# Strassen's product for the values of token tiles 8 and 9, and x of the last token pair prepared a stage later

## The chip, the cores and the metric

The kernel runs on one core of one Trainium2 chip. The metric is the device time of one execution in microseconds: 639.72 us before the change, the median of three runs (639.28 to 639.74). Five engines work side by side, each from a queue of its own and in the order of that queue: TensorE (PE; the load of its weights is shown apart as PEld), VectorE (DVE), ScalarE (ACT), GpSimd (POOL) and SyncE (SP), which does nothing but issue transfers here. One instruction waits for another engine through semaphores, and whatever stands behind it in its queue waits too.

## The reference

2048 tokens of 640 numbers are normalized; a linear attention with 32 heads of 20 numbers and a feed-forward network of width 1536 both read the normalized tokens, and the result is x plus their product. All is float32.

```
xn  = layernorm(x)                                  # 2048 x 640
q, k, v = split(xn @ wqkv)                          # 32 heads of 20
pq, pk = q @ w_phi, k @ w_phi                       # per head
phi_q = concat(softmax(pq), softmax(-pq))           # 40 features of a head
phi_k = concat(softmax(pk), softmax(-pk))
kv  = einsum("bhsf,bhsd->bhfd", phi_k, v)           # sum over all tokens
z   = sum of phi_k over all tokens
s   = (phi_q @ kv) / (phi_q . z + 1e-6) @ wo
g   = silu(gelu(xn @ w1 + b1) @ w2 + b2)
out = x + s * g
```

## The kernel before, in words

The 2048 tokens are 16 tiles of 128. Two neighbouring tiles are a pair: pair q holds tiles 2q and 2q + 1. The 640 inputs of a token are five blocks of 128. A matrix product in float32 is made of three passes in a faster format: every operand is split into a high part (a copy of ACT) and a low part (value minus high part, on DVE or POOL), and PE multiplies high by high, high by low and low by high.

Phase 1 makes keys, values and queries. The key and query weights have `w_phi` folded in. Its plain form is a projection (`project`, matmuls at L401): one tile, five blocks, three passes and two halves of 320 columns, so 30 matmuls. The other form is Strassen's product for a whole pair (`token_pair`, matmuls at L714): blocks 0 and 1 of the even tile's and of the odd tile's inputs are combined beforehand, and so are the weights, and seven products with 54 matmuls give the result for both tiles. The list `QPARTS` (L686) is the order of the seven parts, i = 0 to 6; each ends with a copy on ACT or an addition on POOL or DVE that takes up its bank (L721 on POOL; L725, L728, L731 and L735 on DVE). The last part adds to the bank Z after DVE's addition of part 4 (L728) has read it, so its matmuls wait for that addition. After each part a hook can run, in which the caller places work of other engines: `hooks[i]` is called when part i has been written.

There is no scheduler: the code is written in the order in which each engine does its instructions. So a line that is moved in the code is moved in the queue of every engine that it uses.

A pair's x is prepared by these steps, each of which waits for the one before. `x_in` loads the tokens. `pair_stats` takes mean and variance on DVE (L220) and the power -1/2 on POOL (L223); SP stores mean and factor to DRAM (L326) and loads them back, spread over all partitions (L328, tile `bc`). `load_xr` loads the transposed x of the pair (`xr`, L252 and L253). `pair_sub` subtracts the mean on POOL (L335, two instructions), `pair_mul` multiplies by the factor on DVE (L340). Then `plain` splits it into the operand of the projections (`xp`, and `b` for two blocks of the odd tile; ACT L272, DVE L274, POOL L276). `t_sums` takes Strassen's sums of x (POOL L289, five instructions), and `t_split` splits them (`xd`; ACT L310, POOL L313).

A key or query passes from its bank through `feat1` (DVE: maximum L413, difference L416, minimum L419; POOL: the half with the other sign, L420) and `feat2` (exponential on ACT, L429). A query is then stored to DRAM. A key is finished by `key_fin`: sums and reciprocals on DVE (L437, L469), then the scaling on POOL (L442). `kv_pair` (L481) multiplies the finished keys of a pair with its values in 128 short matmuls, first those of the even tile; they take the heads nearly in order, and from the fourteenth matmul on they read the second half of that tile's values.

The loop from L762 runs over t = 6 to 9. Each turn has a key projection, a value projection and two query projections of tiles 0 to 7, and in turns 7, 8 and 9 the splits and sums of pairs 4, 5 and 6. In turn 9 `value_forms` (`vb`) splits the combined weights of the values that Strassen's product needs. The loop from L823 runs over p = 5, 6 and 7, which are tiles 10 to 15: two key projections, the key-value product of the pair before, and the values of the pair by Strassen's product (`value_pair`), with hooks. For p = 7, `forms` (`qf`) splits the combined query weights in the same way. Four pairs of queries follow by `token_pair` (pairs 4 to 7), and from 238.28 us on the feed-forward network.

Of the kernel before, what the change touches and what calls it, by code (L numbers as in the profile page):

```python
# [15 lines left out]
P = 128  # L16
# [30 lines left out]
def hedgehog_gated_mlp_kernel(ctx: ExitStack, tc: tile.TileContext, x, xt_in, wqk, bd, wv, wo, w1, b1, w2, b2, out_t):  # L47
# [259 lines left out]
    def t_split(q, later=False):  # L307
        dst = xd()[:, :, :, at(q)]
        tt = xrs.pop(q).rearrange("p k (o t) -> p (k o) t", o=2)[:, :9]
        nc.scalar.activation(dst[:, :, 0, :], tt, AF.Copy)  # L310

        def lo(o):
            nc.gpsimd.tensor_tensor(dst[:, o, 1, :], tt[:, o], dst[:, o, 0, :].bitcast(F32), op=OP.subtract)  # L313
        lo(slice(0, 5))
        if later:
            return lambda: lo(slice(5, 9))
        lo(slice(5, 9))
# [440 lines left out]
    XIN = {6: (12, 13), 7: (14, 15)}  # L758
    STATS = {6: (10, 11), 7: (12, 13), 8: (14, 15)}
    x_in(10)  # L760
    x_in(11)
    for t in range(6, 10):  # L762
# [5 lines left out]
        if t == 9:  # L768
            vb = value_forms(sv_raw, [nc.vector, nc.vector, nc.gpsimd, nc.gpsimd])
            next(vb)  # L770
            w_dump(0)
            w_dump(1)
# [3 lines left out]
        if t == 9:  # L776
            next(vb)
        if t > 6:
            feat2(es[t])
            pair_mul(q)  # L780
            pair_plain(q)
            t_sums(q)
        else:
            pair_sub(4)
            fold_w(wqT, range(4, KC), "wq", wq_s)
            feat2(es[t])
        vs[t] = value(t)
        phis[t] = key_fin(es.pop(t))
        pq = project(next(queries), wq_s)
        ef = feat1(pq)  # L790
        if t > 6:
            split_rest = t_split(q, t == 9)
            if t < 9:
                load_xr(q + 1)
        if t == 8:
            sv_raw = [load_raw(sv_dram[k]) for k in range(4)]
        if t == 9:
            next(vb)
# [7 lines left out]
        if t == 9:  # L806
            next(vb)
            next(vb)
            next(vb)
            split_rest()  # L810
            load_xr(7)
        if t in (7, 8):
            pair_sub(q + 1)
        if t < 9:
            store_e(queries_done.pop(0), ef)
        else:
            feat2(ef)
# [4 lines left out]
    qf, later, last_sums = None, [], []  # L822
    for p in range(5, 8):  # L823
# [6 lines left out]
        es[t] = feat1(pk)  # L830
        if p == 6:
            pair_mul(7)
        pk = project(t + 1, wk_s)
        kv_pair(t - 2)
        es[t + 1] = feat1(pk, later)
        if p == 6:
            plain(7, 0, xrs[7][:, :, :P])
            plain(7, 1, xrs[7][:, :, P:], slice(0, 1))
# [7 lines left out]
        def rest(t=t, p=p):  # L846
            if p == 5:
                nc.scalar.dma_start(e_dram[_tok(queries_done.pop(0))], ef)
                next(vb)
                next(vb, None)  # L850
            later.pop(0)()
            if p == 6:
                plain(7, 1, xrs[7][:, :, P:], slice(1, 2), False, True)
                t_sums(7)
            if p == 7:
                next(qf)

        def copied(t=t, p=p):
            feat2(es[t])
            if p == 7:  # L860
                next(qf)

        def first_key(t=t, p=p):
            phis[t] = key_fin(es.pop(t))
            feat2(es[t + 1])

        def second_key(t=t, p=p):
            if p < 7:
                phis[t + 1] = key_fin(es.pop(t + 1))
            else:  # L870
                phis[t + 1] = es.pop(t + 1)
                last_sums.append(key_sums(phis[t + 1]))
            if p == 6:
                t_split(7)

        value_pair(p, {0: lambda: p == 6 and plain(7, 1, xrs[7][:, :, P:], slice(1, 2), True, False), 1: rest, 2: copied, 3: lambda: p == 5 and pair_sub(7), 4: first_key, 6: second_key})
# [712 lines left out]
```

## Time and profile before

| | |
|---|---|
| median of three runs | 639.72 us |
| the profiled execution | 639.93 us |
| its span in the trace | 638.2 us |
| PE busy | 633.0 us, 99% |
| DVE busy | 510.5 us, 80% |
| POOL busy | 432.9 us, 68% |
| ACT busy | 260.5 us, 41% |
| granted clock of PE | nine tenths or more of full speed in each of the 40 slices |

The span runs from the first to the last instruction in the trace; the profiled execution has 1.7 us around it. Busy shares are means over the whole span; the page also cuts the span into 40 slices of about 16 us and shows the busy share of each in tenths. A timeline lists the instructions of one engine in order of time, one group a row: its start in the span, its length, line and operation, output and inputs by the names of the program, and shapes. In square brackets stands how long the engine had been idle before, and what released it.

### The profile page before, as it was taken

What the parts mean: (1) busy time and instruction counts of PE and PEld (TensorE: products, weight loads), DVE (VectorE), ACT (ScalarE), POOL (GpSimd) and SP (SyncE); (2) the same over time, 40 slices, a digit from 0 to 9 for tenths busy, and PEclk for the clock granted to TensorE, in tenths of its full rate; (3) what the DMA queues carried; (4) which work ended last, traced back from release to release, by engine and by line L of the source; (5) the groups of instructions that cost most, each with busy time, mean ns of one, the idle gap of its engine ahead of it and who ended that gap; (6) DMA issues with size and microseconds to landing.
All of it is one profiled execution on the core that took longest, in us unless ns stands there. A gap on an engine that the chain in (4) does not pass through costs nothing.

```text
span 638.2 us, 11443 instructions
## 1 busy us (share of the span) xinstructions
PE 633.0 (99%) x4330; PEld 552.0 (86%) x4330; DVE 510.5 (80%) x784; ACT 260.5 (41%) x389; POOL 432.9 (68%) x377
## 2 busy tenths in 40 slices
PE   9999999999999999999999999999999999999997
PEld 9999999999999998888888888888888888667676
DVE  5886976789788777878989869758798899887585
ACT  3622422334344257243442534842322335455540
POOL 1877466897977764987878776381735678857363
PEclk9999999999999999999999999999999999999999
DMA  8477287394411387449899699797498598969926
GB/s 346 121 234 226 70 286 222 93 299 148 157 43 45 135 273 274 141 95 357 213 280 317 162 368 346 154 318 257 143 238 171 168 187 264 305 184 322 346 71 198
DMA packets 167167, 136.89 MB, mean 214 GB/s; under 512 B 89864, under 2 KB 130824, under 8 KB 166728
## 3 DMA queue, kind: packets, MB, share of 16 engines
q1 hardware_dynamic: 164376, 124.56, 66.0%
q10 hardware_dynamic: 2736, 11.60, 4.8%
q8 instruction: 34, 0.56, 0.4%
q14 instruction: 21, 0.17, 0.1%
HBM read 87.76 MB, written 48.38 MB: 213 GB/s over the span
## 4 chain that ended last, share of the span: by engine, by line
PE 97%; DMA 2%; DVE 0%; SPq 0%; issue 0%; DVEq 0%
PE pB L988 26%; PE pA L401 24%; PE pB L959 23%; PE pB L1190 8%; PE pA L714 6%; PE pB L1116 2%; PE pA L164 2%; PE kv L481 2%; PE qV L714 1%; DMA phT<-phi_t 1%; PE qY L714 1%; DMA xres<-in_xt_dram 1%; PE pA L545 1%; PE pB L1098 0%; PE pA L387 0%; DVE y L1199 0%
## 5 line engine op out<-in xcount | busy, mean ns | idle before, releaser
L988 PE MATMUL pB<-hs,w2s 128*128 128x512 f32 x720 | 165.9, 389 | 0.0
L988 PEld LDWEIGHTS pB<-hs,w2s 128*128 128x128 f32 x720 | 135.0, 188 | 28.8 <-issue 0.8
L959 PE MATMUL pB<-xp,w1s 128*128 128x512 f32 x324 | 81.4, 389 | 0.0
L959 PE MATMUL pB<-xd,w1s 128*128 128x512 f32 x324 | 79.3, 389 | 0.0
L442 POOL TENSOR_TENSOR eq<-eq,rc 128x1280 f32<-128x1280 f32 x16 | 37.9, 2369 | 57.3 <-DVE rc L1050 40.1
L959 PEld LDWEIGHTS pB<-xp,w1s 128*128 128x128 f32 x324 | 60.7, 188 | 12.8 <-ACT x L975 0.3
L959 PEld LDWEIGHTS pB<-xd,w1s 128*128 128x128 f32 x324 | 60.8, 188 | 12.7
L997 DVE TENSOR_TENSOR y<-pB,y 128x512 f32<-128x512 f32 x100 | 63.1, 676 | 1.8 <-PE pB L988 1.8
L964 ACT ACTIVATE pB<-pB,b1t 128x512 f32<-128x512 f32 x48 | 31.8, 662 | 77.4 <-DVE pB L1387 28.9
L429 ACT ACTIVATE e<-e 128x1280 f32<-128x1280 f32 x32 | 40.7, 1273 | 50.1 <-POOL e L420 50.1
L401 PE MATMUL pA<-wk,xp 128*128 128x320 f32 x384 | 59.6, 310 | 0.0
L401 PEld LDWEIGHTS pA<-wk,xp 128*128 128x128 f32 x384 | 56.9, 188 | 0.1
L420 POOL TENSOR_TENSOR e<-nr,e 128x640 f32<-128x640 f32 x32 | 44.7, 1396 | 17.2 <-DVE nr L419 17.2
L1037 POOL TENSOR_TENSOR ez<-eq,zrep 128x1280 f32<-128x1280 f32 x16 | 47.4, 2963 | 6.5 <-DMA eq<-e_dram 6.5
L442 POOL TENSOR_TENSOR e<-e,rc 128x1280 f32<-128x1280 f32 x16 | 37.8, 2367 | 20.4 <-DVE rc L469 20.4
L401 PE MATMUL pA<-wv,xp 128*128 128x320 f32 x240 | 37.0, 310 | 0.0
L509 POOL TENSOR_TENSOR w1s<-raw,w1s 128x640 fp32r<-128x640 f32 (+1 forms) x18 | 25.4, 1412 | 16.0 <-ACT w1s L508 15.9
L139 POOL TENSOR_TENSOR w2s<-raw,w2s 128x640 fp32r<-128x640 f32 x23 | 36.1, 1592 | 0.2 <-ACT w2s L137 0.2
L401 PEld LDWEIGHTS pA<-wv,xp 128*128 128x128 f32 x240 | 35.5, 188 | 0.1
L970 DVE TENSOR_TENSOR hs<-pB,hs 128x512 fp32r<-128x512 f32 x48 | 32.0, 684 | 4.2 <-ACT hs L966 3.8
L137 ACT ACTIVATE w2s<-raw 128x640 fp32r<-128x640 f32 x24 | 17.2, 736 | 43.1 <-DMA xd_dram<-xhi 16.4
L413 DVE TENSOR_REDUCE mx<-pA 128x32 f32<-128x640 f32 x32 | 25.9, 809 | 10.1 <-PE pA L401 9.8
(219 smaller groups left out, 1269.7 us busy)
## 6 DMA issues: line engine op xcount, KB each, us to landing
raw<-in_w_dram SPq DMA_DIRECT2D x42, 320.0 KB, 5.1
e_dram<-e ACTq DMA_DIRECT2D x16, 640.0 KB, 3.9
eq<-e_dram SPq DMA_DIRECT2D x16, 640.0 KB, 5.8
phi_t<-eq SPq DMA_DIRECT2D x64, 160.0 KB, 3.3
phT<-phi_t SPq DMA_DIRECT2D x20, 512.0 KB, 7.5
xt<-in_x_dram SPq DMA_DIRECT2D x16, 320.0 KB, 6.2
xres<-in_xt_dram SPq DMA_DIRECT2D x20, 256.0 KB, 6.7
out_dram<-xres SPq DMA_DIRECT2D x19, 256.0 KB, 4.2
```

Of the source, the lines that this page charges most:

```text
L139: eng.tensor_tensor(sl[:, 1, :], raw, sl[:, 0, :].bitcast(F32), op=OP.subtract)
L401: nc.tensor.matmul(ps[:, hf, :HALF], stat_x(q, o, k, a), ws[k][:, b, hf * HALF:(hf + 1) * HALF], start=n == 0, stop=n == 3 * KC - 1)
L420: rest = lambda: nc.gpsimd.tensor_tensor(e5[:, :, :, 1, :], nr[:, :, :, None].to_broadcast([P, 2, 16, DH]), e5[:, :, :, 0, :], op=OP.subtract)
L429: nc.scalar.activation(ef, ef, AF.Exp)
L442: nc.gpsimd.tensor_tensor(e3, e3, rc[:, :, None].to_broadcast([P, 64, DH]), op=OP.mult)
L714: nc.tensor.matmul(bank[ch], q_x(blk, a, q), p_weight(base, f, w, k)[:, b], start=ch not in seen and n == 0, stop=n == len(mms) - 1, skip_ ...
L959: nc.tensor.matmul(bank[ch][:], tl[:, a, off + wo_:off + wo_ + P], mov(blk, b), start=new and n == 0, stop=n == len(mms) - 1, skip_group_c ...
L970: nc.vector.tensor_tensor(hs[:, 1], ps, hs[:, 0].bitcast(F32), op=OP.subtract)
L988: nc.tensor.matmul(ps[:], ws[i][:, b, d * P:(d + 1) * P], hs[o][i][:, a, :], start=i == n == 0, stop=(i, n) == (GF - 1, 2), skip_group_che ...
L997: nc.vector.tensor_tensor(y, ps[:], y, op=OP.add)
L1037: nc.gpsimd.tensor_tensor(zv, ef, zf, op=OP.mult)
L1190: nc.tensor.matmul(ps[:, mv], w, o[:, mv], start=first and n == 0, stop=last and n == len(steps) - 1, skip_group_check=True)
```

## The change

The values of tiles 8 and 9 are no longer made by two projections in the loop over t, but by a fourth use of `value_pair` at p = 5, behind the key projections of tiles 10 and 11; their key-value product follows it. For that the preparation of the two last pairs is laid out anew. Of pair 6, the multiplication, the splits and the sums go from t = 9 into the hooks of this value pair, and `t_split` and the load of pair 7 into the hooks of the next one. Of pair 7, the statistics (with their store and broadcast load) go from t = 8 into hooks 2 and 4 of the value pair of tiles 10 and 11, the mean subtraction behind it, and the multiplication ahead of the value pair of tiles 12 and 13. In that pair the key-value product of tiles 10 and 11 stands behind the first part. The keys of tiles 8 and 9 are finished a query later than before. At p = 7 the last two `next(qf)`, which split combined query weights, stand in hooks 4 and 5 in place of 1 and 2. Up to L313 line numbers of the two kernels agree; from L315 to L735 of the kernel before, those of the changed kernel are four lower.

The first piece is PE's queue from the key projection of tile 9 on, before. `wk_...` are the key's weights by blocks, `wv` and `wq_...` those of the values and queries, `xp` and `b_...` the split x.

```order
L401 MATMUL pA<-wk_216,xp 128x320 x6
L401 MATMUL pA<-wk_240,xp 128x320 x6
L401 MATMUL pA<-wv,b_1381 128x320 x12
L401 MATMUL pA<-wv,xp 128x320 x18
L401 MATMUL pA<-wq_854,xp 128x320 x6
```

After the change, PE goes from key 9 straight to the queries, and this stands behind the key projection of tile 11. `ws` are combined weights, `xd` Strassen's sums of x, `qY` and `qV` banks of the product, `kv` the bank of the key-value product.

```order
L397 MATMUL pA<-wk_240,xp 128x320 x6
L710 MATMUL pA<-wv,xp 128x320 x6
L710 MATMUL qY<-ws,xd 128x320 x6
L710 MATMUL pA<-wv,xp 128x320 x9
L710 MATMUL qV<-ws,xd 128x320 x6
L710 MATMUL qV<-wv,xp 128x320 x3
L710 MATMUL pA<-wv,xd 128x320 x15
L710 MATMUL pA<-ws,xp 128x320 x6
L710 MATMUL pA<-wv,xp 128x320 x3
L477 MATMUL kv<-e,v 32x40 x64
```

So the 60 matmuls of two projections are gone, 54 of a product have come, and the key-value product stands right behind them.

On DVE the piece before is the first value pair, of tiles 10 and 11. `qu` are the running sums of the product, `qV` and `pA` its banks, `v` the values, `rc` the reciprocals of a key.

```order
L725 TENSOR_TENSOR qu<-qu,qV 128x320
L728 TENSOR_TENSOR v<-qu,pA 128x16x20
L437 TENSOR_REDUCE rc<-e 128x64
L469 RECIPROCAL rc<-rc 128x64
L731 TENSOR_TENSOR v<-qu,pA 128x16x20
L735 TENSOR_TENSOR v<-qu,pA 128x16x20
```

After the change the first value pair is that of tiles 8 and 9, with `xr` and `bc` of pair 6.

```order
L721 TENSOR_TENSOR qu<-qu,qV 128x320
L724 TENSOR_TENSOR v<-qu,pA 128x16x20
L336 TENSOR_TENSOR xr<-xr,bc 128x1280
L727 TENSOR_TENSOR v<-qu,pA 128x16x20
L731 TENSOR_TENSOR v<-qu,pA 128x16x20
L274 TENSOR_TENSOR xp<-xr,xp 128x5x128
L274 TENSOR_TENSOR b_2039<-xr,b_2039 128x2x128
L274 TENSOR_TENSOR xp<-xr,xp 128x3x128
```

The multiplication of pair 6 now stands between the additions that complete the values, where the sums of a key stood in the pair before.

On POOL the piece is the value pair of tiles 10 and 11, before. `ws` are the last two split weights, `e` features, `nr` their minima.

```order
L721 TENSOR_TENSOR qu<-qx 128x320
L652 TENSOR_TENSOR ws<-raw,ws 128x320 x2
L420 TENSOR_TENSOR e<-nr,e 128x32x20
L335 TENSOR_TENSOR xr<-xr,bc 128x5x128 x2
L442 TENSOR_TENSOR e<-e,rc 128x1280 x2
L420 TENSOR_TENSOR e<-nr,e 128x32x20
```

And the same value pair after the change; `pst` are a pair's statistics.

```order
L717 TENSOR_TENSOR qu<-qx 128x320
L416 TENSOR_TENSOR e<-nr,e 128x32x20
L313 TENSOR_TENSOR xd<-xr,xd 128x5x128
L313 TENSOR_TENSOR xd<-xr,xd 128x4x128
L223 TENSOR_TENSOR pst<-pst,mhalf 128x1 x2
L438 TENSOR_TENSOR e<-e,rc 128x1280 x2
L331 TENSOR_TENSOR xr<-xr,bc 128x5x128 x2
L416 TENSOR_TENSOR e<-nr,e 128x32x20
```

The splits of pair 6's sums and the powers of pair 7's statistics have come into it, and the mean subtraction of pair 7 stands behind the scaling of the two keys, where it stood ahead of it.

The diff:

```diff
--- before.py
+++ after.py
@@ -304,17 +304,13 @@
         x_sums(lambda a, b: xr[:, a:b, :P], lambda a, b: xr[:, a:b, P:],
                lambda t: xt_two(xr.rearrange("p k (o t) -> p (k o) t", o=2), t))
 
-    def t_split(q, later=False):
+    def t_split(q, eng=nc.gpsimd):
         dst = xd()[:, :, :, at(q)]
         tt = xrs.pop(q).rearrange("p k (o t) -> p (k o) t", o=2)[:, :9]
         nc.scalar.activation(dst[:, :, 0, :], tt, AF.Copy)
 
-        def lo(o):
-            nc.gpsimd.tensor_tensor(dst[:, o, 1, :], tt[:, o], dst[:, o, 0, :].bitcast(F32), op=OP.subtract)
-        lo(slice(0, 5))
-        if later:
-            return lambda: lo(slice(5, 9))
-        lo(slice(5, 9))
+        for o, e in ((slice(0, 5), nc.gpsimd), (slice(5, 9), eng)):
+            e.tensor_tensor(dst[:, o, 1, :], tt[:, o], dst[:, o, 0, :].bitcast(F32), op=OP.subtract)
 
     def pair_stats(t):
         if t % 2 == 0:
@@ -755,8 +751,8 @@
     wq_f, wq_b, wv_f = [], [], []
     queries_done = list(range(NT // 2))
     queries = iter(range(NT // 2))
-    XIN = {6: (12, 13), 7: (14, 15)}
-    STATS = {6: (10, 11), 7: (12, 13), 8: (14, 15)}
+    XIN = {6: (12, 13), 9: (14, 15)}
+    STATS = {6: (10, 11), 7: (12, 13)}
     x_in(10)
     x_in(11)
     for t in range(6, 10):
@@ -767,34 +763,38 @@
             spill(3)
         if t == 9:
             vb = value_forms(sv_raw, [nc.vector, nc.vector, nc.gpsimd, nc.gpsimd])
-            next(vb)
             w_dump(0)
             w_dump(1)
         if t == 6:
             next(vf[1])
         es[t] = feat1(pk)
-        if t == 9:
-            next(vb)
         if t > 6:
             feat2(es[t])
-            pair_mul(q)
-            pair_plain(q)
-            t_sums(q)
+            if t < 9:
+                pair_mul(q)
+                pair_plain(q)
+                t_sums(q)
         else:
             pair_sub(4)
             fold_w(wqT, range(4, KC), "wq", wq_s)
             feat2(es[t])
-        vs[t] = value(t)
-        phis[t] = key_fin(es.pop(t))
+        if t < 8:
+            vs[t] = value(t)
+        if t < 8:
+            phis[t] = key_fin(es.pop(t))
         pq = project(next(queries), wq_s)
         ef = feat1(pq)
-        if t > 6:
-            split_rest = t_split(q, t == 9)
-            if t < 9:
-                load_xr(q + 1)
+        if t == 9:
+            pair_sub(6)
+        if t > 7:
+            phis[t] = key_fin(es.pop(t))
+        if 6 < t < 9:
+            t_split(q)
+            load_xr(q + 1)
         if t == 8:
             sv_raw = [load_raw(sv_dram[k]) for k in range(4)]
         if t == 9:
+            next(vb)
             next(vb)
         for u in STATS.get(t, ()):
             pair_stats(u)
@@ -804,22 +804,39 @@
         if t == 6:
             next(vf[1])
         if t == 9:
-            next(vb)
-            next(vb)
-            next(vb)
-            split_rest()
-            load_xr(7)
-        if t in (7, 8):
-            pair_sub(q + 1)
+            for _ in range(4):
+                next(vb)
+        if t == 7:
+            pair_sub(5)
         if t < 9:
             store_e(queries_done.pop(0), ef)
-        else:
-            feat2(ef)
         if t == 6:
             kv_pair(4)
         for u in XIN.get(t, ()):
             x_in(u)
     qf, later, last_sums = None, [], []
+
+    def x_last():
+        t_split(6)
+        load_xr(7)
+
+    def first_store():
+        feat2(ef)
+        next(vb)
+
+    def plain_hi(q):
+        for o in range(2):
+            plain(q, o, xrs[q][:, :, o * P:(o + 1) * P], lo=False)
+
+    def x_mid():
+        nc.scalar.dma_start(e_dram[_tok(queries_done.pop(0))], ef)
+        pair_mul(6)
+
+    def x_low():
+        plain(6, 0, xrs[6][:, :, :P], hi=False)
+        plain(6, 1, xrs[6][:, :, P:], hi=False)
+        t_sums(6)
+
     for p in range(5, 8):
         t = 2 * p
         pk = project(t, wk_s)
@@ -828,14 +845,15 @@
             qf = forms(sq_dram, wq_f, wq_b, [nc.vector, nc.vector, nc.vector, nc.gpsimd])
             next(qf)
         es[t] = feat1(pk)
+        pk = project(t + 1, wk_s)
+        if p > 6:
+            kv_pair(t - 2)
+        es[t + 1] = feat1(pk, later)
+        if p == 5:
+            value_pair(4, {1: first_store, 2: lambda: next(vb, None), 4: x_mid, 5: lambda: plain_hi(6), 6: x_low})
+            kv_pair(8)
         if p == 6:
             pair_mul(7)
-        pk = project(t + 1, wk_s)
-        kv_pair(t - 2)
-        es[t + 1] = feat1(pk, later)
-        if p == 6:
-            plain(7, 0, xrs[7][:, :, :P])
-            plain(7, 1, xrs[7][:, :, P:], slice(0, 1))
         if p == 7:
             next(qf)
             next(qf)
@@ -844,23 +862,30 @@
             wq_b.extend(wq_s[2:])
 
         def rest(t=t, p=p):
+            later.pop(0)()
+
+        def copied(t=t, p=p):
+            feat2(es[t])
             if p == 5:
-                nc.scalar.dma_start(e_dram[_tok(queries_done.pop(0))], ef)
-                next(vb)
-                next(vb, None)
-            later.pop(0)()
+                x_last()
+                pair_stats(14)
             if p == 6:
+                plain_hi(7)
+
+        def x_next(p=p):
+            if p == 5:
+                pair_stats(15)
+            if p == 6:
+                plain(7, 0, xrs[7][:, :, :P], hi=False)
+                plain(7, 1, xrs[7][:, :, P:], slice(0, 1), hi=False)
                 plain(7, 1, xrs[7][:, :, P:], slice(1, 2), False, True)
                 t_sums(7)
             if p == 7:
                 next(qf)
 
-        def copied(t=t, p=p):
-            feat2(es[t])
+        def first_key(t=t, p=p):
             if p == 7:
                 next(qf)
-
-        def first_key(t=t, p=p):
             phis[t] = key_fin(es.pop(t))
             feat2(es[t + 1])
 
@@ -870,10 +895,12 @@
             else:
                 phis[t + 1] = es.pop(t + 1)
                 last_sums.append(key_sums(phis[t + 1]))
+            if p == 5:
+                pair_sub(7)
             if p == 6:
                 t_split(7)
 
-        value_pair(p, {0: lambda: p == 6 and plain(7, 1, xrs[7][:, :, P:], slice(1, 2), True, False), 1: rest, 2: copied, 3: lambda: p == 5 and pair_sub(7), 4: first_key, 6: second_key})
+        value_pair(p, {0: lambda: p == 6 and kv_pair(10), 1: rest, 2: copied, 4: x_next, 5: first_key, 6: second_key})
     w1f = w1_forms(w1r)
 
     def early_rest(q, ea):
```

## Rows read from the trace of the kernel before

**Rows 1.** The page: busy time of each engine, and the DMA engines in 40 slices.

```profile
PE 633.0 (99%) x4330; PEld 552.0 (86%) x4330; DVE 510.5 (80%) x784; ACT 260.5 (41%) x389; POOL 432.9 (68%) x377
...
DMA  8477287394411387449899699797498598969926
```

**Rows 2.** Who PE waits for: us in total, times, longest.

```profile
PE pB L1116 <- DMA phT<-phi_t: 0.3, 1, 0.3
```

**Rows 3.** Timeline of PE: start us, length us, instructions, count.

```profile
119.48 4.67 PE L401 MATMUL pA<-wv,xp 128*128 128x320 f32 x30
...
123.98 4.56 PE L401 MATMUL pA<-wq,xp 128*128 128x320 f32 x30
...
128.38 1.92 PE L401 MATMUL pA<-wq,b 128*128 128x320 f32 x12
...
160.60 1.15 PE L714 MATMUL pA<-wv,xp 128*128 128x320 f32 x6
...
168.62 4.56 PE L401 MATMUL pA<-wk,xp 128*128 128x320 f32 x30
...
238.28 1.55 PE L959 MATMUL pB<-xp,w1s 128*128 128x512 f32 x6
```

**Rows 4.** Timeline of DVE, the same stretch.

```profile
129.93 1.48 DVE L437 TENSOR_REDUCE rc<-e 128x64 f32<-128x1280 f32 x1
...
131.91 0.76 DVE L413 TENSOR_REDUCE mx<-pA 128x32 f32<-128x640 f32 x1
...
134.30 0.88 DVE L220 BATCH_NORM_STATS2 st<-xt 128x6 f32<-128x320 f32 x2
...
143.94 1.26 DVE L652 TENSOR_TENSOR ws<-raw,ws 128x640 fp32r<-128x640 f32 x1 [1.99 <-ACT ws L648]
...
166.29 0.49 DVE L728 TENSOR_TENSOR v<-qu,pA 128x320 f32<-128x320 f32 x1
```

**Rows 5.** Timeline of POOL, the same stretch.

```profile
132.74 2.37 POOL L442 TENSOR_TENSOR e<-e,rc 128x1280 f32<-128x1280 f32 x1
...
136.30 2.83 POOL L313 TENSOR_TENSOR xd<-xr,xd 128x640 fp32r<-128x640 f32 x2
...
139.09 1.06 POOL L223 TENSOR_TENSOR pst<-pst,mhalf 128x1 f32<-128x1 f32 x2
...
140.12 1.28 POOL L420 TENSOR_TENSOR e<-nr,e 128x640 f32<-128x640 f32 x1
...
141.36 3.16 POOL L335 TENSOR_TENSOR xr<-xr,bc 128x640 f32<-128x640 f32 x2
...
149.52 3.87 POOL L289 TENSOR_TENSOR xr<-xr 128x256 f32<-128x256 f32 x5 [3.19 <-DVE xp L274]
...
164.79 0.87 POOL L721 TENSOR_TENSOR qu<-qx 128x320 f32<-128x320 f32 x1
...
165.63 1.72 POOL L652 TENSOR_TENSOR ws<-raw,ws 128x320 fp32r<-128x320 f32 x2
```

**Rows 6.** Timeline of ACT, one exponential.

```profile
141.43 1.27 ACT L429 ACTIVATE e<-e 128x1280 f32<-128x1280 f32 x1 [3.78 <-POOL e L420]
```

**Rows 7.** Timeline of DVE, three of the six multiplications of a pair.

```profile
63.24 1.49 DVE L340 TENSOR_TENSOR xr<-xr,bc 128x1280 f32<-128x1280 f32 x1 [3.68 <-POOL xr L335]
...
145.12 2.56 DVE L340 TENSOR_TENSOR xr<-xr,bc 128x1280 f32<-128x1280 f32 x1
...
175.67 3.26 DVE L340 TENSOR_TENSOR xr<-xr,bc 128x1280 f32<-128x1280 f32 x1
```

**Rows 8.** Timeline of SP: two stores of statistics, each with its broadcast load.

```profile
75.96 0.37 SPq L326 DMA_DIRECT2D st_dram<-pst  x1
...
79.17 0.32 SPq L328 DMA_DIRECT2D bc<-st_dram  x1
...
140.18 0.37 SPq L326 DMA_DIRECT2D st_dram<-pst  x1
...
146.69 0.32 SPq L328 DMA_DIRECT2D bc<-st_dram  x1
```

## The prediction

> **What bounds the kernel now.** I read the page first. TensorE (PE) is busy 633.0 of 638.2 us, 99% [rows 1]. Then who PE waits for: once it runs there is one wait, 0.3 us near the end [rows 2]. So the time is the sum of PE's instructions: a matmul less is its own length less, a wait of PE more is its own length more, and everything on the other engines is free as long as it ends before PE asks for it. Last I read, engine by engine, the stretch that the change rewrites (119 to 205 us) [rows 3 to 7], because there the other queues are nearly as full as PE's.
>
> **What it takes off PE.** Two value projections of 30 matmuls go, one token pair of 54 comes. A projection follows the one before it after 4.40 us (123.98 to 128.38), 0.147 us a matmul; a value pair takes 8.02 (160.60 to 168.62), of which 0.1 belongs to the key-value product just before it, since 54 x 0.147 is 7.92 [rows 3]. Saved: 8.80 - 7.92 = 0.88 us. The key-value products keep their number. Uncovered by any wait this gives 639.93 - 0.88 = 639.05 for the profiled execution, which stands 0.2 over the median 639.72.
>
> **What it puts on the path: the values of tiles 8 and 9.** PE's timetable without waits: queries 4 and 5 now start where the value projection of tile 8 stood, 119.5 [rows 3]; key 9 128.3, queries 6 and 7 132.7, keys 10 and 11 141.5, value pair 150.3 to 158.3, its last part (nine matmuls that add to a bank which VectorE, DVE, must have read) from 157.0, the key-value product of tiles 8 and 9 from 158.3. The other engines do the same work in less PE time, so I add up their queues.
>
> DVE is free at 129.9 [rows 4]. Features of a tile cost 2.4 (131.91 to 134.30), the sums with reciprocal of a key 2.0 (129.93 to 131.91). Query 4 ends 132.3, key 8's sums 134.3, then query 5, key 9, query 6: 141.5. GpSimd (POOL) has the pair sums done by 132.6 [rows 5]: half feature of query 4 (1.24), scaling of key 8 from 134.4 (2.37) to 136.8, two splits (2.8) 139.6, three half features (3.7) 143.3, the mean subtraction of pair 6 (3.15) 146.4. ScalarE takes key 9's exponential (1.27, [rows 6]) behind that of query 5 and a store, 142.5 to 143.8. DVE, idle till then, goes on: sums of key 9 145.8, a split of a weight form (1.2, [rows 4]) 147.0, query 7 149.4, another split 150.6, keys 10 and 11 155.4. Its first two additions for the values (0.5 each) end 156.4 [rows 4]. PE's last part needs that at 157.0: 0.6 to spare.
>
> Next in DVE's queue stands the multiplication of pair 6, and behind it the addition that completes the values of tile 8. Their key-value product reads that half from its fourteenth matmul on, 0.3 us in: 158.6. The multiplication took 1.49 with POOL at rest, 2.56 with one POOL instruction beside it, 3.26 with two [rows 7]: in the middle row 1.07 more for a half feature of 1.24. Here POOL's two splits (1.72 after an addition of 0.84, [rows 5]) end about 157.0, so 0.6 is shared. I scale the middle row: 0.5 more, 2.0, to 158.4, and 158.9 after the addition. PE waits 0.3; bounds 0 (1.49) and 1.6 (3.26).
> The Trainium skill (SBUF — State Buffer, Who interferes with whom) says that a DVE instruction with two SBUF inputs and a GpSimd one that reads SBUF block each other, the second for the whole of the first. The middle row agrees nearly: 1.49 and 1.24 make 2.73, it took 2.56. By the rule the multiplication is held until 157.0 and ends 158.5: PE would wait 0.4 instead of 0.3.
>
> **The statistics of the last pair.** They move from tile 8 into the next value pair, with their store, the broadcast load and the mean subtraction behind them. Pair sums began 1.84 after the multiplication's end at the like place (147.68 to 149.52) and took 3.87 [rows 5, 7]: 160.2 to 164.1. POOL goes on: clearing 0.3, addition 0.84 (165.2; DVE's two additions end 166.2, PE's last part of this pair comes at 166.7), half feature 166.5, splits 169.3, two powers (1.0) 170.3. The store and the broadcast that waits for it were issued 3.2 apart when little else ran (75.96 to 79.17) and 6.5 apart at 140.18, in a slice in which the DMA engines were nine tenths busy [rows 1, 8]. At 170 the load of pair 7 has landed (it waits in SyncE's queue, with this store behind it, for the buffer that query 7's store, issued about 155, gives back, so it goes out about 160), and the weight loads stand behind the broadcast, so I take 3.2: issued 173.6. No row shows the broadcast's landing by itself: between 3.2 and 6.5, taken 4.2, nearer the quiet row, 177.8. POOL has scaled keys 10 and 11 by 175.1. Subtraction 181.0, multiplication 2.6 (a half feature beside it) 183.6, two additions 184.6. PE: value pair 160.0 to 168.0 (0.3 late), keys 12 and 13 to 176.8, first part and the key-value product of 10 and 11, now inside the pair, to 179.1, last part 5.8 on, 184.9. So it just fits; I charge 0.1. Bounds: 0, with 1.3 to spare if both trips take 3.2, and 5.3 if both take 6.5. Keys 14 and 15 ask from 186.2 on for the split x that ends about 185.5, covered as long as the term above is.
>
> **The two splits of the query sums.** They go behind the fifth part of the last value pair, so DVE does the pair's two additions ahead of them (a gain that PE cannot use) and key 14's sums behind them. From that pair's start: second addition 6.0, two splits (1.26 each at most, [rows 4]) 8.5, addition 9.0, sums 11.0, POOL's scaling 13.3, its addition for the first query pair 14.2, DVE's two 15.2. PE's last part of that query pair starts at 8.0 + 6.7 = 14.7. Wait 0 to 0.5, taken 0.2, since the splits here are half as wide. The split weights themselves are asked for at 12.4 and 14.7, well after.
>
> Other moves cost nothing as far as rows go: the two token loads of pair 7 (now behind the weight dumps) have 20 us; banks for the projections, which come 4.4 and 8.8 earlier, are read by DVE 1.1 or more before the third projection after; pair 6's key projection starts at 168.0, its x ends about 162.
>
> **Sum.** -0.88 + 0.3 + 0.1 + 0.2 = -0.3: 639.6 for a profiled execution, 639.4 against the median.
>
> **Rivals.**
> 1. All is covered: POOL's splits end earlier and the multiplication takes 1.49. Then 639.05, against the median 638.8. For it: in the like place of before PE shows no wait at all. Against: two of the three rows have POOL beside the multiplication, and DVE has no idle time from 143.8 to 159.
> 2. Slower: the trip of the statistics through DRAM. Place: the last part of the third value pair behind DVE's multiplication of pair 7. Price: if the store alone takes the 6.5 of before's last trip, all is 3.3 later and PE waits 3.0 instead of 0.1: 642.3. It makes the kernel slower by more than 0.2% when store and broadcast together take over some 9.4 instead of 7.4. For it: that 6.5 is this kernel's own latest such trip. Against: what loaded the queues then is not there at 170.
> 3. POOL beside both multiplications throughout, 3.26 each: the key-value product waits 1.6, the later last part 0.4, the query pair 0.5: -0.88 + 2.5 = +1.6, 641.3.
> 4. The products save less or more than counted. PE's matmuls ran back to back in both forms, so I give it little.
>
> **Numbers.** Forecast 62%, rival 1 13%, rival 2 12%, rival 3 10%, rest 3%. About 0.2%, 1.3 us, is what a measurement of this kernel tells from no change. The forecast and rival 1 lie within it, since 0.88 us is 0.14%; rival 2 lies beyond, rival 3 on the border, half each. Faster 4%, within 79%, slower 17%. The range runs from rival 1 to just over rival 3: 638.7 to 641.6; the 5.3 us bound is left outside.
>
> **What would show it.** PE's rows: a token pair of 54 matmuls at about 150.3 and no projection of values after tile 7; the first FFN matmul, at 238.28 before [rows 3], 0.3 earlier. A wait of PE of 0 to 0.5 in the key-value product after that pair, released by DVE's addition, right behind a multiplication of about 2.0. The broadcast issued about 173.6 and the subtraction of pair 7 from about 178; if it starts after 180, PE's last part of the third pair waits and rival 2 holds. Wrong would be a wait at a place not named here, or a first FFN matmul more than 1.3 us from 238.3.

## The result and the profile after

The changed kernel takes 642.11 us (median of six runs, 641.33 to 642.95), the kernel before 639.77 beside it: a ratio of 1.0037, 95% interval 1.0024 to 1.0050. A second series gave 641.12 against 639.29, 1.0030 (1.0018 to 1.0043). The change makes the kernel slower by about 2 us. The forecast was 639.4; the first series lies outside its range (638.7 to 641.6), the second inside.

The page and the list of PE's waits after the change, to be held against [rows 1, 2]:

```profile
PE 632.6 (99%) x4324; PEld 550.7 (86%) x4324; DVE 511.8 (80%) x788; ACT 260.0 (41%) x390; POOL 435.8 (68%) x378
```

```profile
PE pA L710 <- DVE v L724: 1.4, 1, 1.4
PE pB L1143 <- DMA phT<-phi_t: 0.9, 1, 0.9
...
PE pB L1143 <- DVE r L1242: 0.2, 1, 0.2
PE kv L477 <- DVE v L727: 0.2, 1, 0.2
```

PE has six matmuls less, and once it runs four waits where it had one. The largest, 1.4 us, is in the last part of the third value pair, and the last is that of the key-value product of tiles 8 and 9. The two of L1143 are some 32 us from the end (608.2 and 609.4 of 641.0), in code that the change doesn't touch. PE's timeline (start, length, instructions, count) shows the two waits of values and product in place, and the start of the feed-forward network (FFN); the last fence is the key-value product of tiles 6 and 7 before:

```profile
119.02 4.66 PE L397 MATMUL pA<-wq,xp 128*128 128x320 f32 x30
...
157.93 0.47 PE L477 MATMUL kv<-e,v 128*32 128x40 f32 x26
158.57 1.20 PE L477 MATMUL kv<-e,v 128*32 128x40 f32 x102 [0.17 <-DVE v L727]
159.70 1.14 PE L710 MATMUL pA<-wv,xp 128*128 128x320 f32 x6
...
182.43 2.36 PE L710 MATMUL pA<-wv,xd 128*128 128x320 f32 x15
186.16 1.14 PE L710 MATMUL pA<-ws,xp 128*128 128x320 f32 x6 [1.37 <-DVE v L724]
...
239.08 1.55 PE L986 MATMUL pB<-xp,w1s 128*128 128x512 f32 x6
```

```profile
118.15 1.39 PE L481 MATMUL kv<-e,v 128*32 128x40 f32 x128
```

From the end of the key-value product of tiles 6 and 7 to the first FFN matmul it is 239.08 - 119.02 = 120.06 us; before, 238.28 - 119.48 = 118.80 [rows 3]. So this stretch, which holds the whole change, is 1.26 longer. It is cut into three: the product starts again after 1.77 (157.93 to 159.70) where it took 1.32 (118.15 to 119.48 in the profile before), 0.4 more; the last part starts 3.73 after the part ahead of it (182.43 to 186.16), where 15 matmuls of 0.147 are 2.20, 1.5 more and 0.1 in its first row; and 0.88 less for the six matmuls. That is about 1.2. Both waits cost PE some 0.3 more than the idle time that the list gives (1.6 against 1.37, and 0.4 against 0.17): rows overlap where PE doesn't wait (the 15 matmuls are listed with 2.36), and the first row behind a wait is 0.1 longer.

What was late there, on SP, POOL and DVE:

```profile
169.91 0.37 SPq L322 DMA_DIRECT2D st_dram<-pst  x1
173.22 0.33 SPq L324 DMA_DIRECT2D bc<-st_dram  x1
```

```profile
178.56 3.13 POOL L331 TENSOR_TENSOR xr<-xr,bc 128x640 f32<-128x640 f32 x2 [4.01 <-DMA bc<-st_dram]
181.63 1.28 POOL L416 TENSOR_TENSOR e<-nr,e 128x640 f32<-128x640 f32 x1
182.85 0.17 POOL L447 MEMSET v<- 128x32 f32 x1
...
183.11 1.89 POOL L717 TENSOR_TENSOR qu<-qx 128x320 f32<-128x320 f32 x1
```

```profile
181.72 2.55 DVE L336 TENSOR_TENSOR xr<-xr,bc 128x1280 f32<-128x1280 f32 x1 [2.46 <-POOL xr L331]
185.03 0.49 DVE L721 TENSOR_TENSOR qu<-qu,qV 128x320 f32<-128x320 f32 x1 [0.76 <-POOL qu L717]
185.62 0.49 DVE L724 TENSOR_TENSOR v<-qu,pA 128x320 f32<-128x320 f32 x1
```

The store of pair 7's statistics and its broadcast went out almost when the forecast had them (173.2 against 173.6). The subtraction that waits for the broadcast began 5.3 later. The multiplication took 2.55, as forecast. But POOL's addition, 0.87 alone [rows 5], took 1.89: it stood until the multiplication had ended at 184.27. The clearings ahead of it, which read nothing, ran in 0.17 and less under the same multiplication. DVE's two additions came behind POOL's, at 186.1.

The page gives the loss of one execution; 1.26 us of the stretch do not make 2 us. The table sets the profiled executions side by side: the stretch, and the rest from the first FFN matmul to the end of the execution.

| execution | stretch | from the FFN's start to the end | time |
|---|---|---|---|
| before, three executions | 118.80, 118.81, 118.77 | 401.65, 401.56, 401.07 | 639.93, 640.06, 639.15 |
| changed kernel, five | 120.06, 120.06, 119.89, 119.71, 119.89 | 403.60, 402.54, 401.95, 402.84, 403.06 | 642.68, 641.61, 641.29, 641.65, 642.02 |

On average the stretch is 1.13 longer and the rest 1.37; what comes ahead of the stretch is 0.4 shorter. The second loss was not in the forecast.

### The profile page after: what moved, and what is told of

Read it like the earlier page. It is cut to its first block, busy times and chain, and to the rows that moved or that the text cites. A ratio compares the mean times of both kernels' runs of the same rounds, so it can differ in the third digit from the quotient of the medians.

```text
span 641.0 us, 11437 instructions
## 1 busy us (share of the span) xinstructions
PE 632.6 (99%) x4324; PEld 550.7 (86%) x4324; DVE 511.8 (80%) x788; ACT 260.0 (41%) x390; POOL 435.8 (68%) x378
## 4 chain that ended last, share of the span: by engine, by line
PE 93%; POOL 2%; DMA 2%; DVE 1%; issue 0%; ACT 0%; DVEq 0%; SPq 0%; POOLq 0%; ACTq 0%
PE pB L1015 26%; PE pB L986 23%; PE pA L397 21%; PE pB L1217 9%; PE pA L710 6%; PE pB L1143 2%; PE pA L164 2%; PE qV L710 1%; PE kv L477 1%; PE qY L710 1%; DMA xres<-in_xt_dram 1%; DMA bc<-st_dram 1%; PE pA L541 1%; POOL xr L289 1%; DMA st_dram<-pst 1%
## 5 line engine op out<-in xcount | busy, mean ns | idle before, releaser
L993 ACT ACTIVATE hs<-pB 128x512 fp32r<-128x512 f32 x48 | 28.8, 600 | 2.1
L397 PE MATMUL pA<-wq,xp 128*128 128x320 f32 x192 | 29.6, 310 | 0.0
```

The lines of the kernel that those rows point to most:

```text
L397: nc.tensor.matmul(ps[:, hf, :HALF], stat_x(q, o, k, a), ws[k][:, b, hf * HALF:(hf + 1) * HALF], start=n == 0, stop=n == 3 * KC - 1)
```

## The experiments

Each kernel is the changed one with the edit shown, if nothing else is said. Ratios are to the kernel before, timed beside it.

**The changed kernel again** (e1_again, and three executions more).

> The changed kernel once more, for a second profile. Of its 2.3 us over the kernel before, the stretch from the end of the key-value product of tiles 6 and 7 to the first FFN matmul explains 1.26 (120.06 against 118.80 us); PE waits 1.4 in the last part of the third value pair there. Theory A (the statistics of pair 7 come too late, all else is chance of one execution): the stretch is again 119.9 to 120.3, and what lies behind the first FFN matmul comes out near that of before (401.65 us from there to the end of the execution) in some executions, so the median is 641.0 to 641.5. Theory B (the change also lengthens something behind the FFN's start, by 1 us or more, through other transfers): the rest is again 403 or more and the median 642.

1.0030 (1.0018 to 1.0043), stretch 120.06, rest 402.54: the time, 641.12, and the stretch are those of theory A, and the rest lies between the two theories, 0.9 over that of before. The further executions were to tell whether the trip through DRAM varies:

> The changed kernel a third time, one execution with its profile. Over the kernel before it takes 1.8 to 2.3 us more, and only 1.26 of it lie in the stretch up to the FFN in the two profiles so far; executions spread over 640.3 to 644.0, those of the kernel before over 638.5 to 640.5. Theory C (the trip of pair 7's statistics through DRAM takes a different time in each execution and now shows in PE's wait): the stretch and the wait vary from execution to execution, 120 to 122 us, with the time from the issue of the store to the landing of the broadcast. Theory B (the rest is lost at the end, in the last transfers): the stretch is 120.0 to 120.1 each time, and the part behind the FFN's start varies, 402.5 to 404.

Stretch 119.89, 119.71, 119.89; store to broadcast 2.9 to 3.2, broadcast to subtraction 5.3 to 5.5. Theory C fell: the trip is steady. The stretches lie 0.1 to 0.3 below what either theory said. The rest varied from 401.95 to 403.06, nearly as B said (402.5 to 404). Two executions of the kernel before, taken for their profiles (e4_before and e8_before), gave the rows of the table. They too were to tell how far the rest varies: theory A had up to 1 us, theory B under 0.4. The first of them lay 0.1 under the first profile, the second 0.6, more than B gave.

**Powers ahead of the splits** (e2_pow).

```diff
             if p == 5:
-                x_last()
+                load_xr(7)
                 pair_stats(14)
+                pair_stats(15)
...
             if p == 5:
-                pair_stats(15)
+                t_split(6)
```

> Changed kernel, with the statistics of tile 15 taken right behind those of tile 14 and the two splits of pair 6's sums put behind them, so that POOL's two powers stand ahead of the splits (2.8 us). Theory A: the store and the broadcast of pair 7 go out 2.5 to 2.8 us earlier (about 170.5 instead of 173.2), the subtraction starts about 175.7, the multiplication ends by 182, PE's wait of 1.4 in the last part of the third value pair is gone, the stretch to the FFN is 118.4 to 118.6 and the time 1.6 us under the changed kernel. Rival (the wait comes from the multiplication and GpSimd blocking each other there, not from the late broadcast): the multiplication still stands beside GpSimd instructions, the wait stays over 1 us and the time is within 0.5 us of the changed kernel.

The same rows on SP, POOL and DVE:

```profile
167.12 0.37 SPq L322 DMA_DIRECT2D st_dram<-pst  x1
170.12 0.33 SPq L324 DMA_DIRECT2D bc<-st_dram  x1
```

```profile
175.32 3.14 POOL L331 TENSOR_TENSOR xr<-xr,bc 128x640 f32<-128x640 f32 x2 [0.78 <-DMA bc<-st_dram]
178.42 1.28 POOL L416 TENSOR_TENSOR e<-nr,e 128x640 f32<-128x640 f32 x1
...
180.52 1.26 POOL L717 TENSOR_TENSOR qu<-qx 128x320 f32<-128x320 f32 x1 [0.58 <-ACT qx L716]
```

```profile
179.19 1.86 DVE L336 TENSOR_TENSOR xr<-xr,bc 128x1280 f32<-128x1280 f32 x1
182.72 0.49 DVE L721 TENSOR_TENSOR qu<-qu,qV 128x320 f32<-128x320 f32 x1 [1.67 <-PE qV L710]
```

All came 2.8 to 3.2 earlier, DVE's addition now waits for PE, and PE's wait is gone. Stretch 118.28 (expected 118.4 to 118.6), 639.76 against 641.12 (1.4 less, 1.6 expected): 1.0009 (1.0000 to 1.0017). Theory A held for this wait. POOL's addition was still held here (1.26 instead of 0.87), but with 3 us more to spare nothing waited for it.

**The key-value product later as well** (e3_powkv, on the kernel of e2_pow, and once more as e16_powkv).

```diff
-            kv_pair(8)
...
-        value_pair(p, {0: lambda: p == 6 and kv_pair(10), ...
+        value_pair(p, {0: lambda: p < 7 and kv_pair(2 * p - 2), ...
```

> As the run before, and the key-value product of tiles 8 and 9 put behind the first part of the next value pair, so that PE reaches it 0.9 us later. Theory A: PE's wait behind the multiplication of pair 6 (0.2 us, and 0.3 more in which the product's matmuls start slowly) goes too: the stretch to the FFN is 118.0, 0.8 under the kernel before. If nothing is lost behind the FFN's start, the time is 0.6 to 0.9 us under the kernel before (638.9 to 639.2); if theory B holds and 1 us or more is lost there, it is 0.2 to 1 us over it.

> The kernel of the third experiment a second time, for its gain over the kernel before: 0.47 us there, with a stretch 0.81 shorter. Theory A alone: 0.8 under the kernel before; with some of the loss at the end, 0.2 to 0.6 under it again.

The first series: stretch 117.99, 638.82 against 639.29, 0.9991 (0.9982 to 1.0000). The second: 118.46, 639.30 against 639.12, 1.0002 (0.9993 to 1.0010). The stretch is that of the saving alone, 0.81 less, in one execution; in the other POOL ran 0.4 later in the first value pair, and PE lost 0.5 in the last parts of two pairs. The second series missed both expectations, which lay under the kernel before. This is the best variant, and it is not measurably faster than the kernel before.

**The half feature away from the multiplication** (e5_half).

```diff
-        es[t] = feat1(pk)
+        es[t] = feat1(pk, later if p == 6 else None)
...
             later.pop(0)()
+            if p == 6:
+                later.pop(0)()
...
+            if p == 6:
+                plain_hi(7)
             feat2(es[t])
...
-            if p == 6:
-                plain_hi(7)
```

> Changed kernel, where in the third value pair POOL's half feature of key 12 no longer stands beside DVE's multiplication of pair 7, but behind POOL's addition (the high splits of pair 7 go ahead of key 12's exponential so that nothing later is held up). The broadcast is as late as before. Theory A with blocking (while DVE multiplies, a POOL instruction on the same memory stands still, and the other way round; each adds its whole length to the other): the multiplication takes 1.5 instead of 2.55 us, the addition ends at its end plus 0.84, PE waits 0.9 less (0.1 to 0.5 instead of 1.0 to 1.4) and the stretch to the FFN is 119.1 to 119.2 instead of 120.06. Rival (no blocking, only the late broadcast counts): the additions come no earlier, the stretch stays at 120.06.

DVE and POOL in the third value pair:

```profile
181.18 1.49 DVE L336 TENSOR_TENSOR xr<-xr,bc 128x1280 f32<-128x1280 f32 x1 [1.97 <-POOL xr L331]
183.44 0.49 DVE L721 TENSOR_TENSOR qu<-qu,qV 128x320 f32<-128x320 f32 x1 [0.77 <-PE pA L710]
```

```profile
178.00 3.14 POOL L331 TENSOR_TENSOR xr<-xr,bc 128x640 f32<-128x640 f32 x2 [3.51 <-DMA bc<-st_dram]
...
181.33 2.07 POOL L717 TENSOR_TENSOR qu<-qx 128x320 f32<-128x320 f32 x1
183.37 3.10 POOL L416 TENSOR_TENSOR e<-nr,e 128x640 f32<-128x640 f32 x2
```

PE's wait there is gone. The half feature, now behind POOL's addition, no longer slows the multiplication, which took 1.49. The addition began under it and took 2.07: it stood until 182.67 and then needed 0.73. So each of the two is held for as long as the other, begun first, still runs. The Trainium skill (SBUF — State Buffer, Who interferes with whom) says that a VectorE instruction with two inputs in SBUF, the on-chip memory of these tiles, contends with a GpSimd one that reads SBUF, that the shared port is an exclusive lock, and that the order of issue decides who blocks. The trace agrees in both directions: 2.55 for a multiplication behind a half feature, 1.89 and 2.07 for an addition behind a multiplication. Not all of the gain is the half feature's: DVE's two additions ended at 184.52 instead of 186.11, 1.06 by the shorter multiplication and 0.54 because the broadcast was that much earlier in this execution (subtraction from 178.00 instead of 178.56). PE asked for them at 184.58, so with the broadcast as late as before some 0.5 of the wait would have stayed (an estimate), as expected. The stretch is 119.69, not 119.1: 0.5 was spent further on, in waits of 0.6 for the split sums of pair 7 and 0.2 for a key, both on POOL, which does the same work later. The times do not show the gain: 1.0044 (1.0031 to 1.0057), and the profiled execution (640.02) is the shortest of the six.

**Statistics where they were** (e6_early).

```diff
-    XIN = {6: (12, 13), 9: (14, 15)}
-    STATS = {6: (10, 11), 7: (12, 13)}
+    XIN = {6: (12, 13), 7: (14, 15)}
+    STATS = {6: (10, 11), 7: (12, 13), 8: (14, 15)}
...
-                pair_stats(14)
...
-            if p == 5:
-                pair_stats(15)
```

> Changed kernel with the statistics of pair 7 back in the stage of tile 8, where the kernel before had them, and all else of the change kept. Theory A: the wait in the third value pair goes (-1.6), but in the stage of tiles 8 and 9, where the two value projections no longer give DVE 8.8 us of PE's time, DVE's 2.3 us more make PE wait some 1.5 for a bank before query 5 or 6, and the first addition chain of the value pair comes later: stretch to the FFN 119.6 to 120.4, about as the changed kernel. Rival (DVE had room there, and moving the statistics was needless): 118.2 to 118.5 and 1.6 us under the changed kernel.

```profile
138.72 2.00 PE L397 MATMUL pA<-wq,b 128*128 128x320 f32 x12 [1.37 <-DVE e L412]
```

The row is PE's: it waits 1.37 for a bank that DVE empties too late, the wait of the third pair is gone, and the stretch is 120.53, 0.1 over what theory A said: 1.0049 (1.0033 to 1.0064). So the move bought something: without the two projections DVE has no room for the statistics in that stage.

**The splits of the query weights back** (e7_splits, on the kernel of e3_powkv), and moved alone in the kernel before (e13_b_splits).

```diff
             later.pop(0)()
+            if p == 7:
+                next(qf)
...
             feat2(es[t])
+            if p == 7:
+                next(qf)
...
-            if p == 7:
-                next(qf)
```

> The kernel of the third experiment (stretch 117.99), with the last two splits of the combined query weights back behind the first and second part of the last value pair. The prediction put 0 to 0.5 us of wait on their move, taken 0.2; the profile of the changed kernel shows none. Theory A: the stretch stays at 118.0 within 0.1, and the time with it. Rival (the move was worth something, since DVE is freed for the last pair's additions): PE waits at the last part of that pair and the stretch is 118.3 or more.

> The kernel before, with only the last two splits of the query weights moved behind the fourth and fifth part of the last value pair (the last edit of the change by itself). Both theories: the stretch up to the FFN is 118.8, since nothing of it is on PE's path. Theory D (the end of the kernel hangs on transfers, and any difference in order shifts them; the kernel before happens to lie well): the time is 0.4 to 1.5 us over the kernel before all the same. Theory E (the loss behind the FFN's start belongs to the Strassen part or to its lateness): the time is that of the kernel before within 0.3.

DVE in the last value pair with the splits back, PE there, and then the same place of PE in e3_powkv:

```profile
199.19 1.16 DVE L648 TENSOR_TENSOR wqb<-raw,wqb 128x320 fp32r<-128x320 f32 x1
200.28 1.56 DVE L648 TENSOR_TENSOR ws<-raw,ws 128x320 fp32r<-128x320 f32 x1
201.76 0.47 DVE L721 TENSOR_TENSOR qu<-qu,qV 128x320 f32<-128x320 f32 x1
202.34 0.49 DVE L724 TENSOR_TENSOR v<-qu,pA 128x320 f32<-128x320 f32 x1
```

```profile
200.46 2.36 PE L710 MATMUL pA<-wv,xd 128*128 128x320 f32 x15
202.88 1.14 PE L710 MATMUL pA<-ws,xp 128*128 128x320 f32 x6
203.86 0.60 PE L710 MATMUL pA<-wv,xp 128*128 128x320 f32 x3
```

```profile
200.26 2.36 PE L710 MATMUL pA<-wv,xd 128*128 128x320 f32 x15
202.47 1.04 PE L710 MATMUL pA<-ws,xp 128*128 128x320 f32 x6
203.34 0.60 PE L710 MATMUL pA<-wv,xp 128*128 128x320 f32 x3
```

The list of waits shows nothing there, but PE needs 3.40 (200.46 to 203.86) where it needed 3.08, since DVE's second addition ends at 202.83, behind the two splits. That is 0.3, all that the stretch, 118.32, has over 117.99: the rival held, and with the other waits gone the move is worth 0.3. The time, 1.0013 (1.0004 to 1.0021) after 0.9991 and 1.0002, is higher by more than that; why is open. In the kernel before the move alone (the key of tile 14 is finished behind the splits there, a part later) gave a stretch of 118.80 and 1.0003 (0.9995 to 1.0012): no difference.

**No wait for the store** (e12_notrip).

```diff
-                              st_dram[q].rearrange(...).partition_broadcast(P))
+                              st_dram[min(q, 6)].rearrange(...).partition_broadcast(P))
```

> Changed kernel in which pair 7's x is normalized with the broadcast statistics of pair 6, which lie in DRAM long before: the store and the load are still issued in the same places of SP's queue, but the load waits for no store (it leaves out the use of pair 7's own statistics). Theory C: the broadcast lands 3 us earlier, about 175.5, PE's wait in the third pair goes (stretch 118.2 to 118.5), and the spread of the executions shrinks to that of the kernel before (2 us or less), the time 1.5 to 2.2 under the changed kernel. Theory B: the time falls by 1.6 at most and stays 0.5 or more over what the stretch says, with the spread of the changed kernel (3 us and more).

```profile
169.95 0.37 SPq L322 DMA_DIRECT2D st_dram<-pst  x1
170.42 0.41 SPq L324 DMA_DIRECT2D bc<-st_dram  x1
```

The load goes out right behind the store, the subtraction starts at 174.54, the wait is gone and the stretch is 118.32. The time is 1.0006 (0.9997 to 1.0016), 1.5 us under the changed kernel's second series. The spread, 638.42 to 640.99, is 2.6 us: between what B and C said.

**What lies behind the FFN's start** (e14_b_delay and e15_b_mem, both from the kernel before).

```diff
+            if q == 7 and i == 1 and not out:
+                mms = mms[:1] * 9 + mms
```

```diff
-    const.tile([P, 16], F32, name="align")
+    algn = const.tile([P, 16], F32, name="align")
+    nc.gpsimd.memset(algn[:], 0.0)
```

> The kernel before with nine matmuls of the last query pair repeated (each overwrites the one before it), so that PE comes 1.32 us later to the FFN and nothing else is changed. If lateness costs at the end: the time is 2 us or more over the kernel before. Theory D or E: 1.3 over it (1.0 to 1.7; D allows 0.5 more).

> The kernel before with one more POOL instruction at its start, the clearing of a tile that nothing reads. Stretch 118.8 by all theories. Theory D: 0.3 to 1.5 us over the kernel before, or under it; theory E: within 0.3 of it.

The delay (stretch 120.12, 1.32 more) cost 1.0029 (1.0017 to 1.0040), 1.1 to 2.6 us: 1.3 fits, and so would 2. The idle instruction cost nothing that shows: 1.0004 (0.9995 to 1.0013). With e13 this speaks against theory D, though the intervals of both reach 0.8 us. Rest behind the FFN's start in these: 401.14 (e13), 402.27 (e14; 0.4 of it lies outside the trace, where the span is 2.1 short of the time and elsewhere 1.7), 401.25 (e15).

## Why the forecast was wrong, step by step

**The saving** was right. With the waits out of the way the stretch was 0.81 shorter (e3) against 0.88.

**The key-value product of tiles 8 and 9** was right: forecast 0.3, and 0.4 on PE's path in four of the five executions of the changed kernel (0.6 in the other), though the list shows 0 to 0.3 idle. The multiplication ahead of it took 1.99 (2.0 forecast) and the addition behind it ended at 158.5 (158.9).

**The query splits** were taken at 0.2 and cost nothing; left where they were, they would have cost 0.3 once the waits ahead were gone (e7).

**The statistics of the last pair** are the step that failed: "Subtraction 181.0, multiplication 2.6 (a half feature beside it) 183.6, two additions 184.6", with a charge of 0.1. It cost 1.3 to 1.6. Two of its terms were short. The broadcast took 5.3 from its issue to the subtraction, where 4.2 had been taken between 3.2 and 6.5: 0.7 of it was left at the end of the subtraction. And "two additions" left out that POOL's addition stands ahead of them and on the same memory: the prediction let the half feature slow the multiplication, but not the multiplication hold the addition. That is 0.8 of the 186.1 against 184.6. By these rows either alone would have left PE waiting some 0.8 (an estimate). In e2 and e12 the subtraction began 3.2 and 4.0 earlier, far more than the 0.7, and the wait went wholly. No run takes away the hold of the addition alone: in e5 it is still there (2.07), and what went is the half feature, which the forecast had counted. So its 0.8 is read from rows, and no run proves it by itself. That a POOL instruction is held by one of DVE could have been read from the trace of before. A half feature, 1.28 at 140.12 [rows 5], began there 0.54 after DVE's split of 143.94 to 145.20 [rows 4] and took 1.85; the prediction read the row only for what it did to DVE's multiplication, and as 1.24:

```profile
144.48 1.85 POOL L420 TENSOR_TENSOR e<-nr,e 128x640 f32<-128x640 f32 x1
```

**Rival 2** had the place and the sign, with 12%: PE waits in that last part behind the multiplication. Its condition was wrong: store and broadcast together took 8.65 (3.3 and 5.3), not over 9.4, the subtraction began at 178.6, not after 180, and PE waited all the same because of the held addition. That its 642.3 is near 642.11 is chance: it had all of the loss in this wait, which holds 1.5 of it.

**The other rivals** did not come: the multiplications took 1.99 and 2.55, not 1.49 (rival 1) and not 3.26 each (rival 3), and the saving was as counted (rival 4).

**Beyond the stretch** the sum had nothing, and the changed kernel loses 0.5 to 2.2 us there in every profiled execution against the mean of before. The forecast range would have held the time without it: the terms as measured up to the FFN make 639.72 - 0.88 + 0.4 + 1.5 = 640.7, an estimate. One place where PE waits there, in the changed kernel and then in an execution of the kernel before:

```profile
604.48 2.79 PE L1143 MATMUL pB<-phT,bdk 120*64 120x512 f32 x12
608.16 1.08 PE L1143 MATMUL pB<-phT,bdk 120*64 120x512 f32 x4 [0.89 <-DMA phT<-phi_t]
```

```profile
603.22 4.51 PE L1116 MATMUL pB<-phT,bdk 120*64 120x512 f32 x20
```

The same 20 matmuls run through in one execution and wait for a load in the other. But this holds little of the loss: from their start to the next matmul it is 5.97, 4.44, 4.51, 4.71 and 5.33 in the five of the changed kernel, and 5.08, 4.44 and 4.44 in the three of before, 0.3 more on average. Ahead of it, from the FFN's start, 0.5 more goes (365.4 to 366.2 against 365.1 to 365.5). The largest part, 0.6, lies behind the issue of the last store, SP's last row, again of the changed kernel and of before:

```profile
637.34 0.33 SPq L1228 DMA_DIRECT2D out_dram<-xres  x1
```

```profile
635.36 0.33 SPq L1201 DMA_DIRECT2D out_dram<-xres  x1
```

From the end of this row to the end of the span, 641.0 and 638.2, it is 3.3 against 2.5; over all executions 2.8 to 3.3 against 2.4 to 2.5. Why is not settled. It isn't the trip of the statistics (steady), and no edit of the kernel before disturbed the end by more than 0.8 (e13, e15). Lateness of the FFN alone may cost from nothing to 1.2 us (e14), but behind its last store e14 has 2.4 like the kernel before, and e5 and e6, which are late too, had a rest of 401.3. Variants of the changed kernel that are not late had 401.3 to 402.5, and behind the last store 2.4 (e3, e7) to 2.8 (e2, e12, e16). The profiled executions of e5 and e6 were among their shortest, 1.8 and 0.8 us under the medians of their series, so a single profile says little here.

## What to carry to other kernels

Where a change of 0.9 us on PE's path takes room from DVE and POOL, add up their queues to the last instruction that PE waits for, and let every pair of a DVE instruction with two SBUF inputs and a POOL instruction beside it that reads SBUF cost the sum of both, in either order, and let what follows the second start behind that sum. A chain through DRAM (store, broadcast) that was sized from rows of another stage, here 7.4 where it took 8.65, is not covered by 0.3 us to spare: issue its head ahead of work that nobody waits for, as e2 did with two splits. Below 0.3%, profile several executions of both kernels before a difference is put down to one place.

## What the runs showed that was not expected

- A POOL addition of 0.87 us took 1.89 and 2.07 beside a DVE multiplication that had begun first, and the multiplication 2.55 instead of 1.49 behind a half feature of 1.28.
- The broadcast of 512 numbers to 128 partitions took 5.1 to 5.5 us from its issue to the subtraction in ten executions where it was waited for, and 2.7 to 3.3 passed between the issue of the store and its own.
- The same kernel's part behind the FFN's start varied by 1.65 us over five executions, without a difference in the order of its instructions.
